# Block 4's scores, K^T V and state moved behind the second unit of products

## The chip, the cores and the metric

The kernel runs on one core of one Trainium2 chip. The metric is the device time of one execution in microseconds (us). Before the change it is 753.96 us, the median of three runs (753.72 to 754.04).

## What is computed

Two stages follow each other. The first is retention, a causal attention without softmax whose scores decay with the distance; the second is a feed-forward layer with the maximum of three products in its middle.

```python
scores = q @ k.T / sqrt(64)                      # batch 8, heads 8, sequence 576, head size 64
ret = scores * gamma[h] ** (i - j)  where i >= j, else 0
x = (ret @ v), heads side by side                # 4608 tokens x 512
h = maximum(maximum(x @ w1, x @ w2), x @ w3)     # 4608 x 768
out = h @ w_out                                  # 4608 x 512
```

All is float32 but the four weight matrices, which come as 64-bit floats and are taken apart into float32 on the chip.

## The kernel before

**Tiles.** The 4608 tokens are 36 blocks of 128, and four blocks are one tile of 512 tokens, so there are nine tiles. For a block, retention needs: its q, k and v loaded; v scaled by decay factors on GpSimd (`decay`, L243); q and k transposed (`transposes`, L256: on TensorE against the identity for the first blocks, into two PSUM banks `kt` and `qt` which ScalarE copies to SBUF at L274); the scores (`scores`, L276: 16 matmuls into two PSUM banks, s0 and s1, which VectorE multiplies by the causal mask into `st`); K^T V (`state`, L346: 8 matmuls recorded as 16 rows, into one bank `kv`); and the running state (`keep`, L357: VectorE reads `kv`, scales or adds it). `values` (L377) then multiplies the masked scores by v, adds the part of the state, and VectorE writes the result into `xT`, the input of the feed-forward layer, tile by tile.

**PSUM.** Three pools share it. `ps_r` has four buffers and serves retention: transposes, scores, K^T V and values. `ps_x` and `ps_y` have two each and serve the products of the feed-forward layer. Each buffer holds 512 float32 values per partition. A tile taken from a pool waits until an earlier holder has been read for the last time.

```python
    ps_r = ctx.enter_context(tc.tile_pool(name="ps_r", bufs=4, space=PSUM))
```

**The first tile.** While tile 0 runs through the feed-forward layer, the weights are still being loaded and converted. Its products come in nine units, three for each pair of 128 weight columns: pair 0 with w1, w2, w3, then pair 1, then pair 2. A unit is two calls of `up_plain` (L781), one for each column block; each is four products of 128 x 512 (recorded as eight rows, L786). The first result of a pair is copied to `h` by ScalarE (L793), the second and third are joined by VectorE's maximum (L791). The conversion of the weights is a generator (`convert_all`, L616) that hands out one step at a time: VectorE cuts out exponent and fraction (L632, L641), ScalarE makes the low word and the power of two (L634, L640, L643), VectorE puts fraction and sign in (L646, L650) and multiplies (L658). Each finished piece asks for one more piece from HBM (L661), so the 'bits' arrive in the order of the pieces, all over one DMA queue. The first three pairs of pieces (one pair for each unit) are converted one piece at a time, 128 x 512; from the fourth on two together, 128 x 1024. In the second unit `ffn` (L818) emits four conversion steps between a product and its maximum:

```python
                for fb in (2 * fp, 2 * fp + 1):
                    maximum, = up_plain(t, h, fb, i)
                    ...
                        convert(4 if (fp, i) == units[1] else 2)
                        maximum()
```

**The order of the work.** The tool that builds the program keeps the order in which the code emits instructions (L124), so every engine works through its instructions in program order. The order around the change is written out by hand in `steps` (L942): a list of 12 places for each tile, where retention of the next tile is dealt out; after each place `ffn` emits its next unit (L986 to L989). For tile 0 the first unit is `first_ups` (L800), which also holds block 3's values, then block 4's `decay` and `transposes`. In the lines of `steps` for t == 1, a is block 4, b block 5, c block 6 and d block 7. Place 1 holds block 4's scores, K^T V and state and lies between the first unit and the second; place 2 holds block 5's transposes and lies between the second and the third.

Of the kernel before, what the change touches and what calls it, by code (L numbers as in the profile page):

```python
# [81 lines left out]
def kernel(  # L82
# [698 lines left out]
    def up_plain(t, h, fb, i, *parts):  # L781
        ps = (ps_x, ps_y)[fb % 2].tile([P, NT], FP32, tag="xy"[fb % 2], name="up")

        def products(a, b):
            for dc in range(NDC):
                nc.tensor.matmul(ps[:, a:b], lhsT=w_sb[i, fb][:, dc * P:(dc + 1) * P], rhs=xT[t][:, dc, a:b],  # L786
                                 start=dc == 0 and a == 0, stop=dc == NDC - 1, skip_group_check=len(parts) > 0)

        def maximum():
            if i > 0:  # L790
                nc.vector.tensor_tensor(h[:, fb, :], h[:, fb, :], ps[:], op=ALU.max)  # L791
            else:
                nc.scalar.copy(h[:, fb, :], ps[:])  # L793

        ends = [0, *parts, NT]
        steps = [partial(products, a, b) for a, b in zip(ends, ends[1:])]
        steps.pop(0)()
        return (*steps, maximum)
# [143 lines left out]
    def steps(t):  # L942


        todo = [[] for _ in range(3 * CPT)]

        def at(n, *what):
            for step, *args in what:
                if step is values:
                    if args[0][0] < NG:  # L950
                        todo[n].append(partial(values, *args))
                elif args[0] < NG:
                    todo[n].append(partial(soon, partial(step, *args)) if step is load else partial(step, *args))

        if t == 1:
            a, b, c, d = range(CPT, 2 * CPT)
            at(0, (load, b))
            at(1, (scores, a), (state, a), (keep, a))
            at(2, (transposes, b), (decay, b), (load, c), (load_weights, 2))
            at(3, (scores, b), (load_blocks, d, 0))  # L960
            at(4, (decay, c), (load_blocks, d, 1, 2))
            at(5, (values, [a, b], [b, c]), (load_blocks, d, 3), (load, d))
            at(6, (keep, c), (transposes, c), (load_blocks, d + 1, 0))
            at(7, (transposes, d), (decay, d), (load_blocks, d + 1, 1, 2))
            at(8, (scores, c), (scores, d), (load_blocks, d + 1, 3), (load, d + 1))
            at(9, (load_blocks, d + 2, 0, 1))
            at(10, (decay, d + 1), (load_blocks, d + 2, 2))
            at(11, (values, [c, d], [d]), (load_blocks, d + 2, 3), (load, d + 2),
               (transposes, d + 1))
            return todo  # L970
        for n in range(0, CPT, 2):
            a, b, m = CPT * t + n, CPT * t + n + 1, 6 * (n // 2)
            first_pair = a == BY_CHUNKS
            s = m + 2 if first_pair else m + 1
            at(m - (t == 2 and n > 0), (transposes, b))
            if first_pair:
                at(m, (decay, b), (load, a + 2), (carry, a))
            at(s, (scores, a), (scores, b), (load, b + 2))
            at(s + 1, (decay, a + 2))
            at(s + 2, (decay, b + 2))  # L980
            at(s + 3, (values, [a, b]), (transposes, a + 2), (load, a + 4))
        return todo

    for t in range(N // NT):
        work = ffn(t)
        for todo in steps(t + 1):  # L986
            for step in todo:
                step()
            next(work, None)  # L989
# [51 lines left out]
```

## Time and profile before

| what | value |
|---|---|
| time, median of 3 | 753.96 us |
| span of the profiled execution | 751.6 us |
| granted TensorE clock, mean | 1.00 |
| TensorE matmul rows of 'up' (L786, all tiles) | 208 rows, 563 ns mean length (they overlap) |
| share of the chain in lines L762 (later tiles' products) | PE a 19%, b 16%, c 8%, d 5%, e 5% |
| DMA busy share, by tens of us | 0.9 or more in each of the first six, 0.61 in the seventh |

The profile names engines PE (TensorE; PEld is its weight load), DVE (VectorE), ACT (ScalarE), POOL (GpSimd) and SP (the queue that issues the transfers). A row of a timeline gives the start and length in us, the engine, the line, the operation, the tiles written and read, how many instructions are merged, and in brackets the idle time of the engine before it with what ended it. A busy TensorE row's end is a model; its start is not.

### The profile page before, as it was taken

What the parts mean: (1) busy time and instruction counts of PE and PEld (TensorE: products, weight loads), DVE (VectorE), ACT (ScalarE), POOL (GpSimd) and SP (SyncE); (2) the same over time, 40 slices, a digit from 0 to 9 for tenths busy, and PEclk for the clock granted to TensorE, in tenths of its full rate; (3) what the DMA queues carried; (4) which work ended last, traced back from release to release, by engine and by line L of the source; (5) the groups of instructions that cost most, each with busy time, mean ns of one, the idle gap of its engine ahead of it and who ended that gap; (6) DMA issues with size and microseconds to landing.
All of it is one profiled execution on the core that took longest, in us unless ns stands there. A gap on an engine that the chain in (4) does not pass through costs nothing.

```text
span 751.6 us, 16577 instructions
## 1 busy us (share of the span) xinstructions
PE 744.8 (99%) x6736; PEld 609.4 (81%) x6736; DVE 509.9 (68%) x856; ACT 319.7 (43%) x645; POOL 83.1 (11%) x103
## 2 busy tenths in 40 slices
PE   8999999999999999999999999999999999999998
PEld 7645545588888888888888888888888888888887
DVE  3997987857866765686567746775667656763662
ACT  3754531155245433644254335542554245414441
POOL 3210112002000100011010101010101010100000
PEclk9999999999999999999999999999999999999999
DMA  9995842515152414242333224232424141000001
GB/s 227 229 248 132 227 88 73 96 17 99 44 94 41 87 48 97 47 77 52 81 78 67 62 66 91 48 67 67 88 38 92 44 93 37 1 30 29 0 1 57
DMA packets 230204, 59.30 MB, mean 79 GB/s; under 512 B 210800, under 2 KB 228848, under 8 KB 230128
## 3 DMA queue, kind: packets, MB, share of 16 engines
q1 hardware_dynamic: 228720, 57.91, 35.4%
q8 instruction: 53, 0.87, 0.5%
q10 hardware_dynamic: 1408, 0.33, 0.2%
q14 instruction: 23, 0.19, 0.1%
HBM read 48.76 MB, written 9.44 MB: 77 GB/s over the span
## 4 chain that ended last, share of the span: by engine, by line
PE 97%; DMA 1%; SPq 1%; ACT 0%; DVE 0%; issue 0%
PE a L762 19%; PE b L762 16%; PE dx L559 11%; PE up L786 11%; PE c L762 8%; PE dz L559 6%; PE d L762 5%; PE e L762 5%; PE sk L309 3%; PE down L773 3%; PE dy L559 3%; PE o L426 2%; PE o L433 2%; PE s L287 1%; PE o L395 1%; PE kv L312 1%
## 5 line engine op out<-in xcount | busy, mean ns | idle before, releaser
L750 DVE TENSOR_TENSOR part<-part 128x512 f32<-128x512 f32 x161 | 111.2, 691 | 107.6 <-ACT part L747 105.2
L747 ACT COPY part<-b 128x512 f32<-128x512 f32 x115 | 67.3, 585 | 154.9 <-PE b L762 154.9
L750 DVE TENSOR_TENSOR h<-h,part 128x512 f32<-128x512 f32 x115 | 79.5, 691 | 29.1 <-ACT h L747 25.2
L786 PE MATMUL up<-xT,w 128*128 128x512 f32 (+2 forms) x208 | 84.8, 563 | 0.0
L747 ACT COPY part<-a 128x512 f32<-128x512 f32 x92 | 53.8, 585 | 49.4 <-PE a L762 48.9
L786 PEld LDWEIGHTS up<-xT,w 128*128 128x128 f32 x208 | 37.7, 190 | 41.4 <-issue 38.4
L762 PE MATMUL a<-s,w 128*128 128x256 f32 x276 | 70.9, 380 | 0.0
L762 PE MATMUL b<-s,n 128*128 128x256 f32 x276 | 70.8, 379 | 0.0
L191 ACT ACTIVATE vraw<-vraw,gk 128x64 f32<-128x64 f32 x208 | 65.5, 346 | 1.5 <-DMA vraw<-in_v_dram 1.5
L762 PEld LDWEIGHTS b<-s,n 128*128 128x128 f32 x276 | 52.5, 190 | 7.1
L762 PEld LDWEIGHTS a<-s,w 128*128 128x128 f32 x276 | 52.4, 190 | 7.1
L529 POOL TENSOR_TENSOR H<-h 128x256 f32<-128x256 f32 x24 | 20.2, 841 | 310.1 <-DVE h L750 310.1
L762 PE MATMUL c<-xT,w 128*128 128x256 f32 x184 | 49.1, 389 | 0.0
L762 PE MATMUL d<-s,w 128*128 128x256 f32 x184 | 47.2, 379 | 0.0
L762 PE MATMUL b<-xT,n 128*128 128x256 f32 x184 | 47.2, 379 | 0.0
L326 POOL TENSOR_TENSOR s<-s,gs_of 64x512 f32<-64x512 f32 x21 | 22.4, 1068 | 211.2 <-DVE s L324 209.2
L559 PE MATMUL dx<-To,H 128*128 128x256 f32 (+1 forms) x204 | 44.9, 370 | 0.0
L762 PE MATMUL e<-xT,w 128*128 128x256 f32 x184 | 43.5, 379 | 0.0
L762 PE MATMUL a<-xT,n 128*128 128x256 f32 x184 | 43.5, 379 | 0.0
L559 PEld LDWEIGHTS dx<-To,H 128*128 128x128 f32 x204 | 36.7, 190 | 4.8
L762 PEld LDWEIGHTS e<-xT,w 128*128 128x128 f32 x184 | 35.0, 190 | 5.1 <-DVE s L324 0.2
L762 PEld LDWEIGHTS d<-s,w 128*128 128x128 f32 x184 | 35.0, 190 | 4.7
(122 smaller groups left out, 1287.3 us busy)
## 6 DMA issues: line engine op xcount, KB each, us to landing
bits<-in_moe_w_dram SPq DMA_DIRECT2D x36, 256.0 KB, 5.7
out_dram<-osb SPq DMA_DIRECT2D x35, 256.0 KB, 2.1
kraw<-in_k_dram SPq DMA_DIRECT2D x32, 256.0 KB, 3.1
vraw<-in_v_dram SPq DMA_DIRECT2D x32, 256.0 KB, 3.5
qraw<-in_q_dram SPq DMA_DIRECT2D x224, 32.0 KB, 2.2
kxraw<-in_k_dram SPq DMA_DIRECT2D x224, 32.0 KB, 2.1
bits<-in_moe_w_out_dram SPq DMA_DIRECT2D x6, 512.0 KB, 5.1
qraw<-in_q_dram SPq DMA_DIRECT2D x6, 256.0 KB, 5.8
```

The costliest lines, as they stand in the source:

```text
L191: scaling.popleft()()
L309: nc.tensor.matmul(s[half(c), h, :], lhsT=kT[half(c), h, :], rhs=qT[half(c), h, :], start=True, stop=True)
L326: nc.gpsimd.tensor_tensor(new, new, factor, op=ALU.mult)
L426: nc.tensor.matmul(o[m][half(c), n, u, :], lhsT=vds[g][half(m), h, :], rhs=sts[g][half(m), h, :], start=n == 0 and u == 0, stop=place(g, m ...
L433: nc.tensor.matmul(o[m][half(c), n, u, :], lhsT=stacks[g][half(m), h, :], rhs=qks[g]["q"][half(m), h, :], start=False, stop=True, skip_gro ...
L529: urgent.append(lambda: (pool(s3, a11, a21, op=ALU.subtract), pool(s4, a12, s2, op=ALU.subtract)))
L559: nc.tensor.matmul(o, lhsT=hS[n](fp)[:, m * P:(m + 1) * P], rhs=late["T"][n][:, fp, cols], start=first and fp == order[0] and (m == 0 or l ...
L747: nc.scalar.copy(of[step], ps[step[0]][:])
L750: nc.vector.tensor_tensor(of[dst], a, b, op=op)
L762: nc.tensor.matmul(ps[chain][:, e, :], lhsT=factor(w, 2 * fp + e), rhs=xS[t][x], start=n == 1 and e == 0, stop=ends, skip_group_check=True)
L773: nc.tensor.matmul(b[:], lhsT=h[:, fb, m * P:(m + 1) * P], rhs=w_sb["out", fb], start=(fb == 0), stop=(fb == NF - 1))
L786: nc.tensor.matmul(ps[:, a:b], lhsT=w_sb[i, fb][:, dc * P:(dc + 1) * P], rhs=xT[t][:, dc, a:b], start=dc == 0 and a == 0, stop=dc == NDC - ...
```

## The change

The list of place 1 is put at the head of place 2. Scores, K^T V and state of block 4 are then emitted after the second unit's products, conversions and maxima, directly ahead of block 5's transposes. Nothing else moves, and no instruction is added or removed. The second unit then stands between block 4's transposes, whose copies ScalarE has still to make, and the scores that read these copies.

```diff
         if t == 1:
             a, b, c, d = range(CPT, 2 * CPT)
             at(0, (load, b))
-            at(1, (scores, a), (state, a), (keep, a))
-            at(2, (transposes, b), (decay, b), (load, c), (load_weights, 2))
+            at(2, (scores, a), (state, a), (keep, a), (transposes, b), (decay, b), (load, c), (load_weights, 2))
             at(3, (scores, b), (load_blocks, d, 0))
```

## The prediction

> **What bounds the kernel now.** I read the page's busy table and chain first, to see whether any engine but TensorE can set the end.
>
> ```profile
> span 751.6 us, 16577 instructions
> ...
> PE 744.8 (99%) x6736; PEld 609.4 (81%) x6736; DVE 509.9 (68%) x856; ACT 319.7 (43%) x645; POOL 83.1 (11%) x103
> ...
> PE 97%; DMA 1%; SPq 1%; ACT 0%; DVE 0%; issue 0%
> ```
>
> TensorE is the chain. The question is then where it stands still, so I asked for its waits from 33 us to the end (columns: total us, times, longest). There is one answer:
>
> ```profile
> PE s L287 <- ACT qT L274: 0.8, 1, 0.8
> ```
>
> It lies at the place that the change touches: block 4's scores wait for the copy of its transposed q. After it TensorE never waits again. So nothing later can swallow a delay made here: a microsecond lost or won near 40 us arrives at the end whole. The timeline of TensorE around it (start, length, work, idle before) gives the order of the work:
>
> ```profile
> 31.70 0.60 PE L273 MATMUL kt<-ident,kraw 128*128 128x128 f32 x4
> 32.14 0.60 PE L273 MATMUL qt<-ident,qraw 128*128 128x128 f32 x4
> 33.52 1.16 PE L287 MATMUL s<-qT,kT 64*128 64x128 f32 x16 [0.78 <-ACT qT L274]
> 34.61 0.68 PE L354 MATMUL kv<-vd,kraw 64*64 64x64 f32 x16
> 35.22 7.13 PE L786 MATMUL up<-xT,w 128*128 128x512 f32 x16
> 42.19 0.60 PE L273 MATMUL kt<-ident,kraw 128*128 128x128 f32 x4
> 42.63 0.60 PE L273 MATMUL qt<-ident,qraw 128*128 128x128 f32 x4
> 43.07 7.03 PE L786 MATMUL up<-xT,w 128*128 128x512 f32 x16
> ```
>
> The fifth line is the second unit (columns 0 and 1 of the first weight pair, i = 1); the first two are block 4's transposes, the sixth and seventh block 5's. I use starts, since the ends overlap the next start. Pieces by starts: a set of four transposes 0.44 us (42.63 - 42.19), scores 1.09, K^T V 0.61, the unit 6.97 (42.19 - 35.22).
>
> The third thing to know is what VectorE does in that stretch, because it masks the scores. Its timeline:
>
> ```profile
> 34.80 1.28 DVE L203 TENSOR_TENSOR st<-s,causal 128x512 f32<-128x512 f32 x2
> 36.00 0.41 DVE L362 TENSOR_TENSOR state<-kv,gs 128x256 f32<-128x256 f32 x1
> ...
> 40.89 1.41 DVE L658 TENSOR_TENSOR w<-mant,expo 128x512 f32<-128x512 f32 x1
> 42.40 0.69 DVE L632 TENSOR_SCALAR expo<-bits 128x1024 int32<-128x1024 int32 x1
> 43.01 0.69 DVE L641 TENSOR_SCALAR frac<-bits 128x1024 int32<-128x1024 int32 x1
> 43.80 1.23 DVE L646 SCALAR_TENSOR_TENSOR mant<-frac,mant 128x1024 f32<-128x1024 int32 x1
> 44.95 0.68 DVE L791 TENSOR_TENSOR h<-h,up 128x512 f32<-128x512 f32 x1
> ```
>
> and ScalarE's row for the same weights, which waited for the transfer that brings them:
>
> ```profile
> 42.40 1.29 ACT L634 ACTIVATE mant<-bits,one 128x1024 f32<-128x1024 uint32 x1 [4.13 <-DMA bits<-in_moe_w_dram]
> ```
>
> The reader is to see two things. The masks stand ahead of the second unit's conversions on VectorE now. And the last conversions of that unit (L632, L641, L646 on 128x1024, the first piece pair of the next weight columns) can't begin before 42.40, when their bits land; only after them comes the unit's second maximum, L791 at 44.95, although its product was finished at about 42.3.
>
> **What the Trainium skill says.** "Perfetto Trace Analysis", section "Tensor Engine Instruction (MATMUL, LD_WEIGHTS)", says that ends of TensorE rows are estimated while ACT and DVE are strict FIFO. The trace agrees: TensorE's lengths overrun the next start (0.60 against 0.44), and the maximum at 44.95 stood behind conversions. "PSUM — Partial Sum Buffer", section "Specifications (TRN2)", gives eight banks of 512 fp32 values per partition. The kernel's pools take 4 + 2 + 2 of them; the trace shows no bank numbers. "TensorE: Matmul & The Clock Gate", section "Part 1: The HAM clock gate", says that an idle window of about 3.4 us, whose phase is free, halves the clock. In this trace four transposes took 1.06 us at 4.15 us and 0.60 at 31.70, so a slower start is there; a drop inside the run is not.
>
> **The change part by part.**
>
> *Removed: the wait of 0.78 us.* TensorE will go from block 4's transposes straight to the second unit. That needs the unit's weights: by the timeline of VectorE the product (L658) of its first column ended at 32.29 and of its second at 34.21. The transposes hand over at 32.14 + 0.44 = 32.58, and the second column is needed 3.5 us later, so neither is waited for. The output banks come from the other two pools and were free by then. Unit: 32.58 to 39.55. Scores: 39.55 to 40.64. K^T V: to 41.25. First half of block 5's transposes: to 41.69. Up to here TensorE is 42.63 - 41.69 = 0.94 us ahead of before (0.78 of wait and the pipeline's refill).
>
> *Moved: the masks and the state, on VectorE.* They leave their place at 34.80 and go behind all of the second unit's conversions and both its maxima. Nothing that stood behind them is late: the first five conversions come 1.6 us sooner, but end in a wait for the bits of 42.40. The transfers are issued in the same order and none of them waits on VectorE for its buffer until after that, so I take 42.40 unchanged. Then 43.01, 43.80, the maximum at 44.95, and the first mask 0.61 later (a maximum at 51.92 was followed by a mask at 52.52): 45.56 to 46.24.
>
> *Added: a wait for a bank.* The pool of scores, K^T V and transposes has four banks. Block 4's two score banks and its K^T V bank stay taken until VectorE has read them; the transposed k of block 5 takes the fourth. The transposed q of block 5 has no bank until the first mask is done. Before, that mask ended at about 35.5, seven microseconds before q's turn. Now it ends at 46.24; a release from VectorE to TensorE cost 0.05 us (a mask that ended at 18.00, matmuls at 18.05). So q's transposes start at 46.29 in place of 42.63: **3.66 us later**, a stall of 4.6 us from 41.69. Behind them in TensorE's queue stands everything: the third unit, block 5's scores, all later units; they wait with it.
>
> *Costs nothing:* the state update (0.41 us of VectorE) and the second mask follow the first mask while TensorE transposes and runs the third unit for 7 us. Two steps merging into one list adds no instruction. Block 4's masked scores and state are first used at 65.05. ScalarE copies block 5's q after 46.9 instead of 46.27; its scores come 7 us after. The conversions of the next columns end at about 50.3 in place of 49.5, but their unit starts at 51.12 + 3.66 = 54.8.
>
> Sum: 753.96 - 0.94 + 4.60 = 753.96 + 3.66 = **757.6 us**.
>
> **The rivals.**
>
> *Only the removed wait counts* (not slower). If a bank were free for q, or VectorE reached the masks before 42 us, the change would give its 0.94 us: 753.96 - 0.94 = 753.0, which is within 0.2%. For it speaks that TensorE shows no bank wait anywhere after 33 us. Against it: the count of four banks leaves no spare, and the conversion ahead of the masks has the transfer's wait in it. 0.07.
>
> *The bank wait and a slower clock after it.* A stall of 4.6 us exceeds the page's idle window of 3.4 us, and with a free phase holds a whole one in (4.6 - 3.4)/3.4 = 35% of the cases. By estimate from the page the work then runs at half speed for most of a window or two, which loses 1.2 to 3.4 us, most likely 1.6: 757.6 + 1.6 = 759.2. For: the four transposes at 4.15 took 1.06 us. Against: no lower clock within this span. 0.28.
>
> *A shorter bank wait.* If the bits land 2 us sooner than at 42.40, the stall shrinks alike: 755.6. DMA engines are busy throughout, and the issue order is the same, so there is little for it: 0.03.
>
> **How the numbers follow.** The full wait at full clock has 0.62 and is the forecast, 757.6. Its own uncertainty is the refill after a stall and the transfer's landing, some 0.5 us either way. The range 756.6 to 760.4 holds it and most of the slower clock; it leaves out the two smaller cases and the slower clock's tail, under 2 in 10. Slower by over 0.2% (beyond 755.5): 0.62 + 0.28 + most of 0.03, so 0.92. Within 0.2%: 0.06. Faster: 0.02, for a removed wait with a knock-on that I don't see.
>
> **What would show it.** In the changed profile: the second unit's products start near 32.6 with no wait; the scores near 39.6; an idle stretch of some 4.5 us on TensorE ahead of the transposed q of block 5, ended by VectorE's L203; the first mask near 45.6 right behind L791 at 44.95; the third unit near 46.7; no other new wait. A dip of the granted clock near 46 would be the slower rival. Without the idle stretch, or with the masks ahead of 42.4, the forecast is wrong.

## The result, and the profile after

| | before | after |
|---|---|---|
| time, median | 753.90 us (753.70 to 754.04, 6 runs) | 758.11 us (755.55 to 759.02, 6 runs) |
| ratio | | 1.0054, 95% interval 1.0039 to 1.0069 |
| span of the profiled execution | 751.6 us | 756.7 us (that execution took 759.02) |
| mean granted TensorE clock of that execution | 1.00 | 0.995 |

The change costs 4.2 us. The forecast was 757.6, with a range of 756.6 to 760.4. Where the time went shows in three views. First the waits of TensorE from 30 us to the end (total us, times, longest), which have a single answer again, but another than before:

```profile
PE qt L273 <- ACT kT L274: 3.1, 1, 3.1
```

The timeline of TensorE shows where it lies:

```profile
31.66 0.60 PE L273 MATMUL kt<-ident,kraw 128*128 128x128 f32 x4
32.09 0.60 PE L273 MATMUL qt<-ident,qraw 128*128 128x128 f32 x4
32.53 7.03 PE L786 MATMUL up<-xT,w 128*128 128x512 f32 x16
39.49 1.16 PE L287 MATMUL s<-qT,kT 64*128 64x128 f32 x16
40.58 0.68 PE L354 MATMUL kv<-vd,kraw 64*64 64x64 f32 x16
41.20 0.66 PE L273 MATMUL kt<-ident,kraw 128*128 128x128 f32 x4
44.98 1.11 PE L273 MATMUL qt<-ident,qraw 128*128 128x128 f32 x4 [3.13 <-ACT kT L274]
45.88 9.31 PE L786 MATMUL up<-xT,w 128*128 128x512 f32 x16
55.12 1.16 PE L287 MATMUL s<-qT,kT 64*128 64x128 f32 x16
```

The second unit follows block 4's transposes without the old wait, and block 5's k is transposed at 41.20, 0.99 us sooner than before. Then TensorE stands still for 3.1 us, counted from the modelled end of that row, until block 5's q may be transposed. From there two rows are longer than before: q's transposes take 0.90 us from start to start in place of 0.44, and the third unit 9.24 in place of 6.96. The windows of one us say why (each row gives the window and its length, the busy time of PE, PEld, DVE, ACT and POOL with the number of instructions after x, then the granted clock, the DMA share and GB/s):

```profile
43.00:44.00 1.00, 0.00 (x0) 0.00 (x0) 1.00 (x2) 0.97 (x2) 0.00 (x0) 0.82 1.04 249
44.00:45.00 1.00, 0.02 (x1) 0.02 (x1) 1.00 (x3) 0.93 (x2) 0.00 (x0) 0.50 1.07 270
...
49.00:50.00 1.00, 1.00 (x2) 0.34 (x1) 0.00 (x0) 1.00 (x2) 0.00 (x0) 0.50 1.06 239
50.00:51.00 1.00, 1.00 (x3) 0.53 (x2) 0.00 (x0) 1.00 (x2) 0.00 (x0) 0.77 1.09 245
```

The clock fell to half during the stall and came back near 50.5. The sum closes: q starts 2.35 us later than before (44.98 - 42.63), its transposes lose 0.46 and the third unit 2.28, so block 5's scores start 5.09 us later (55.12 - 50.03). The profiled execution took 759.02, which is 5.06 above the 753.96 of the profiled execution before. Nothing after 55 us gave any of it back.

Last, the other two engines. VectorE:

```profile
40.98 0.69 DVE L632 TENSOR_SCALAR expo<-bits 128x1024 int32<-128x1024 int32 x1 [0.21 <-DMA bits<-in_moe_w_dram]
41.59 0.69 DVE L641 TENSOR_SCALAR frac<-bits 128x1024 int32<-128x1024 int32 x1
42.38 1.23 DVE L646 SCALAR_TENSOR_TENSOR mant<-frac,mant 128x1024 f32<-128x1024 int32 x1
43.52 0.68 DVE L791 TENSOR_TENSOR h<-h,up 128x512 f32<-128x512 f32 x1
44.12 1.28 DVE L203 TENSOR_TENSOR st<-s,causal 128x512 f32<-128x512 f32 x2
```

and ScalarE:

```profile
40.97 1.26 ACT L634 ACTIVATE mant<-bits,one 128x1024 f32<-128x1024 uint32 x1 [2.90 <-DMA bits<-in_moe_w_dram]
42.13 1.14 ACT L640 ACTIVATE expo<-expo,top 128x1024 f32<-128x1024 int32 x1
43.30 1.15 ACT L643 ACTIVATE expo<-expo,inf 128x1024 int32<-128x1024 f32 x1
44.36 0.57 ACT L274 COPY kT<-kt 128x512 f32<-128x512 f32 x1
```

Both stood behind the conversions that wait for their bits, as forecast. But the first mask ended near 44.80 (44.12 and 0.68 for one of the two) and the copy of block 5's k at 44.93, and q started at 44.98: the profile names the copy as the releaser. The built programs agree. The first matmul of q's transposes waits for a transfer and for one engine, and that engine changed from VectorE (DVE) to ScalarE (Activation):

```
-L273 Matmult qt<-ident,qraw 128x128 [waits DMAHW0_49,DVE_49]
+L273 Matmult qt<-ident,qraw 128x128 [waits DMAHW0_49,Activation_49]
```

In the kernel before, q got a bank of block 4's scores; after the change the builder gave it the bank of its own block's k, so it waits until ScalarE has copied k out.

### The profile page after: what moved, and what is told of

It reads as the page before. It is cut to its first block, busy times and chain, and to the rows that moved or that the text cites. A ratio compares the mean times of both kernels' runs of the same rounds, so it can differ in the third digit from the quotient of the medians.

```text
span 756.7 us, 16578 instructions
## 1 busy us (share of the span) xinstructions
PE 747.9 (99%) x6736; PEld 610.1 (81%) x6736; DVE 510.4 (67%) x856; ACT 319.6 (42%) x645; POOL 83.8 (11%) x103
## 4 chain that ended last, share of the span: by engine, by line
PE 96%; SPq 2%; DMA 1%; ACT 1%; issue 0%; DVE 0%; POOL 0%; POOLq 0%; ACTq 0%
PE a L762 18%; PE b L762 16%; PE dx L559 11%; PE up L786 9%; PE c L762 8%; PE dz L559 5%; PE e L762 5%; PE d L762 5%; PE sk L309 3%; PE down L773 3%; PE dy L559 3%; PE o L426 2%; PE o L433 2%; SPq L241 1%; PE o L395 1%; PE s L287 1%
## 5 line engine op out<-in xcount | busy, mean ns | idle before, releaser
L786 PE MATMUL up<-xT,w 128*128 128x512 f32 (+2 forms) x208 | 87.0, 575 | 0.1
L762 PEld LDWEIGHTS b<-xT,n 128*128 128x128 f32 x184 | 35.0, 190 | 4.8
```

The lines of the kernel that those rows point to most:

```text
L762: nc.tensor.matmul(ps[chain][:, e, :], lhsT=factor(w, 2 * fp + e), rhs=xS[t][x], start=n == 1 and e == 0, stop=ends, skip_group_check=True)
```

## The experiments

The comparisons are with the kernel before, run on the same chip beside each. It took 753.97 us beside the first filler, the bank for q, the copies first and the masks first; 753.95 beside the changed kernel run again, the second filler, the late conversion and the scores moved alone; 754.18 beside the other three. A ratio stands with its 95% interval. Two questions were open: how much of the 4.2 us is the stall and how much the clock, and what it is that q waits for.

### The clock: keep TensorE busy in the stall

In `transposes`, with FILLER = 15:

```diff
+            if g == CPT + 1 and n == "q":
+                warm(FILLER)
             pt = pool.tile([P, NP, C], FP32, tag=tag, name=n + "t")
```

> The changed kernel with fifteen extra products of the identity with itself on TensorE ahead of block 5's q transposes (into a bank of the third pool that is free; their result is used by nobody, the rest is computed as before). At full clock two recorded rows of 0.11 us are one such product, so they fill 3.3 of the 3.8 us of the stall and don't move its end. Theory 'the stall also costs clock': the granted clock stays 1.0, the third unit takes 7.0 us in place of 9.3, and the time is 753.9 + 2.3 = 756.2, some 2 us less than the changed kernel's 758.1. Rival 'the whole loss is the wait, and the clock costs nothing': 758.1 as without the filler.

Measured: 757.58 us, ratio 1.0047 (1.0034 to 1.0059), clock 1.00 in all five runs. The clock behaved as its theory says, but the time was 1.4 us above the expected. In the profiled execution the bits landed only at 42.82, and q started at 46.87 in place of 44.98. So executions and chips differ in the landing, and the comparison needed the changed kernel on the same chip:

> The changed kernel once more, beside the one with the filler. Theory 'the stall also lowers the clock': above the filler's time of the same chip by 1.2 to 2.7 us (one to two windows of 3.4 us at half speed, less what falls into the stall), and the profile shows a stretch at 0.50 after the stall and a third unit of more than 7.1 us. Rival 'the loss is the wait alone, and only the landing of the bits makes runs differ': the same time as with the filler within 0.4 us.

> As the filler before, now beside the changed kernel on the same chip: fifteen products of the identity ahead of block 5's q transposes, of which nobody uses the result. Theory 'the stall also lowers the clock': clock 1.0, and 1.2 to 2.7 us below the changed kernel. Rival 'the loss is the wait alone': no difference. In both, q starts about 4 us after k.

Measured on one chip: 758.51 us without the filler (1.0067, 1.0054 to 1.0080), 756.80 with it (1.0040, 1.0027 to 1.0052). All five runs without it had a mean clock of 0.995 to 0.998, all with it 1.00, so the filler kept the clock up. The medians differ by 1.7 us. As the clock's part this is a rough figure: there are five runs of each, and the landing moves by more than a microsecond (in the two profiled executions the bits landed at 42.37 and 41.09, so q started 5.28 us after k without the filler and 4.07 with it, where some 4 had been expected in both). Within one trace the clock's part does not hang on the landing. From start to start, against the kernel before, q's transposes and the third unit lost 0.46 and 1.06 us in this profile of the changed kernel, 1.5 us together, and 2.7 us (0.46 and 2.28) in the first. What is left with the filler, 2.85 us (756.80 - 753.95), is put down to the stall. The filler itself ends near 45.1 and can't show a stall shorter than that. The timelines of TensorE show both parts. Without the filler:

```profile
41.13 0.66 PE L273 MATMUL kt<-ident,kraw 128*128 128x128 f32 x4
46.41 1.12 PE L273 MATMUL qt<-ident,qraw 128*128 128x128 f32 x4 [4.61 <-ACT kT L274]
47.31 8.08 PE L786 MATMUL up<-xT,w 128*128 128x512 f32 x16
55.33 1.16 PE L287 MATMUL s<-qT,kT 64*128 64x128 f32 x16
```

With it (the lines of this kernel are numbered three higher):

```profile
41.09 0.66 PE L276 MATMUL kt<-ident,kraw 128*128 128x128 f32 x4
41.58 3.51 PE L159 MATMUL warm<-ident 128*128 128x128 f32 x30
45.16 0.66 PE L276 MATMUL qt<-ident,qraw 128*128 128x128 f32 x4
45.65 7.03 PE L789 MATMUL up<-xT,w 128*128 128x512 f32 x16
52.62 1.16 PE L290 MATMUL s<-qT,kT 64*128 64x128 f32 x16
```

The third unit is 8.08 long where the clock is lowered for a part of it, and 7.03 at full clock. The start of q follows the landing: in the changed kernel's two profiles ScalarE's L634 began at 40.97 and 42.37 and q at 44.98 and 46.41; in the two filler profiles at 42.81 and 41.09, and q at 46.87 and 45.16. Always 4.0 to 4.1 us lie between, the three activations and the copy.

### A bank for q

```diff
             pool, tag = (ps_r, "r") if g >= CPT else (ps_x, "x")
+            if g == CPT + 1 and n == "q":
+                pool, tag = ps_y, "y"
```

> The changed kernel, but the transposed q of block 5 is put in a bank of the third pool, which is free at that time. Nothing in the order of any engine changes: the masks and the copy of the transposed k still come after the conversions that wait for their bits. Theory 'q waits for a bank and for nothing else': no stall above 0.2 us ahead of q, clock 1.0, and the gain of the removed wait alone: 753.9 - 0.9 = 753.0. Rival 'q waits for its data or for VectorE's or ScalarE's work itself': a stall of 3 to 4 us stays, 757 to 758.

Measured: 753.58 us, ratio 0.9995 (0.9986 to 1.0003). No order was touched, VectorE masked at 45.66 and ScalarE copied k at 45.91, as late as ever, yet q went right behind k. So the bank is what q waits for. Of the 0.9 us that should be won, 0.4 arrived, and the interval holds 1, so even that is not clear of noise. The one wait that is left on TensorE tells where the rest went (lines numbered two higher; the wait is of the fifth unit, at 58.06):

```profile
PE up L788 <- DVE w L660: 0.4, 1, 0.4
```

That unit came 0.4 us too soon for its converted weights: from start to start, it began 7.52 us after the fourth (50.54) in place of 6.97.

### Which release: the copy of k, or the masks

Both pieces were emitted ahead of the second unit's last four conversion steps, one at a time; TensorE's order is that of the changed kernel in each. The steps so moved are taken out of the list of places, which the excerpts below do not show. In `ffn`, behind the product of the unit's second column, the copies first (the masks are held back until after the maximum):

```diff
+                    if (fp, i) == units[1] and fb % 2:
+                        spread.append(True)
+                        for step in (scores, state, keep):
+                            step(CPT)
+                        spread.clear()
+                        transposes(CPT + 1)
...
                         maximum()
+                        chore(len(urgent))
```

> The changed kernel, with block 4's scores and K^T V and block 5's transposes emitted ahead of the second unit's last four conversion steps, but the masks and the state update left behind them. TensorE's order is that of the changed kernel; ScalarE copies the transposed k of block 5 ahead of the conversions that wait for the bits; VectorE masks as late as in the changed kernel. Theory 'ScalarE's copy of k gives the bank that q waits for' (the trace names it): q starts 0.6 us after k's transposes, near 42.3, third unit right behind: 753.9 - 0.3 = 753.6, clock 1.0. Rival, the forecast's own 'VectorE's first mask gives the bank': the stall stays, 757 to 758.

Or the masks first, with the transposes left in place 2:

```diff
+                    if (fp, i) == units[1] and fb % 2:
+                        scores(CPT)
+                        state(CPT)
+                        keep(CPT)
```

> The changed kernel, with block 4's scores, K^T V, masks and state update emitted ahead of the second unit's last four conversion steps. TensorE's order is that of the changed kernel; VectorE masks before the conversions that wait for the bits; ScalarE copies the transposed k of block 5 as late as in the changed kernel. Theory 'any of the four banks will do, the first to be read': q takes a bank of the scores, whose mask ends near 41.3, and does not stall: 753.0, plus up to 1 us because VectorE now stands idle for the scores and its conversions come 2 us later than before, so 753.0 to 754.0. Rival 'only ScalarE's copy of k frees q's bank': the stall stays, 757 to 758.

Measured: copies first 754.86 us (1.0014, 1.0007 to 1.0020), masks first 754.07 (1.0002, 0.9993 to 1.0010). With the copies first, q keeps k's bank and starts behind the copy, four microseconds ahead of the masks. TensorE, then VectorE:

```profile
41.26 0.66 PE L273 MATMUL kt<-ident,kraw 128*128 128x128 f32 x4
42.59 0.66 PE L273 MATMUL qt<-ident,qraw 128*128 128x128 f32 x4 [0.68 <-ACT kT L274]
```

```profile
46.77 1.28 DVE L196 TENSOR_TENSOR st<-s,causal 128x512 f32<-128x512 f32 x2
```

With the masks first, the program gives q a bank of the scores; q started at 42.23, although ScalarE copied k only at 48.20. So either release will do, and in the changed kernel it was the copy.

Neither kernel gained in the end. With the copies first, q started at 42.59, as in the kernel before (42.63): the wait for the copy, which was expected, took back what the removed wait gave. The rest was lost to the weights of the fourth and fifth unit. VectorE masked only at 46.77, after a conversion that stood 1.74 us waiting for ScalarE, and came late with what those units need:

```profile
51.44 7.13 PE L786 MATMUL up<-xT,w 128*128 128x512 f32 x16 [0.23 <-DVE w L658]
58.76 7.13 PE L786 MATMUL up<-xT,w 128*128 128x512 f32 x16 [0.19 <-DVE w L658]
65.82 1.97 PE L395 MATMUL o<-st,vd 128*64 128x128 f32 x32
```

The idle times in brackets, from modelled ends, show about half of it. From start to start the fourth unit came 1.39 us after block 5's scores (50.05) in place of 1.09, and the values 14.38 after the fourth unit in place of 13.93 (65.05 - 51.12). That is 0.75 us, nearly all of the 0.79 by which the profiled execution (754.75) was longer than that of the kernel before. With the masks first, VectorE stood idle for 2.64 us waiting for the scores, and the fourth and fifth unit waited 0.86 and 0.65 us for L658 in the profiled execution, which at 755.41 was the slowest of its thirteen.

### The conversion that waits for its transfer

```diff
-                        convert(4 if (fp, i) == units[1] else 2)
+                        convert(4 if (fp, i, fb) in ((0, 1, 0), (0, 2, 0)) else 2)
```

> The changed kernel with the two conversion steps that wait for the bits moved from the second unit's second column to the third unit's first column, behind the masks, the state and the transposes' copies. Theory 'the transfer of the bits, ahead of the masks and the copy in VectorE's and ScalarE's order, makes the stall': q's bank is one of the scores', read near 42, so q waits 0.4 us at most: 753.4 to 754.0 (the upper end if the conversions of later units keep TensorE waiting as in the kernel with the masks first). Rival 'masks behind the second unit are late whatever stands ahead of them': a stall of over 2 us, above 756.

Measured: 753.41 us, ratio 0.9992 (0.9983 to 1.0000). The stall is gone, with the masks at 40.70 and the copy of k at 41.65, and q is not held up (the third row starts 0.49 behind the second):

```profile
40.35 0.68 PE L354 MATMUL kv<-vd,kraw 64*64 64x64 f32 x16
40.96 0.66 PE L273 MATMUL kt<-ident,kraw 128*128 128x128 f32 x4
41.45 0.64 PE L273 MATMUL qt<-ident,qraw 128*128 128x128 f32 x4
41.93 7.03 PE L786 MATMUL up<-xT,w 128*128 128x512 f32 x16
```

So the move behind the second unit is harmless by itself. It hurts because two conversion steps stand in front of what releases the banks. They delay the release by their wait for the transfer and by their own work, and this experiment takes both away together. The wait is not all of it. In the first profile of the changed kernel VectorE stood only 0.21 us for the bits (L632 at 40.98; 2.45 us in the second), and from there ScalarE needed 3.4 us for its three activations before it could copy k.

I also tried to bring the transfer forward by loading block 5's v one place later (`(load, b, "kq")` at place 0, `(load, b, "v")` at place 1):

> The changed kernel with block 5's v loaded one place later, so that the bits that VectorE and ScalarE wait for are issued ahead of it. Theory 'q starts 4.0 us after the bits land, or after VectorE comes to them': VectorE comes to them near 40.0, the two activations that need it end near 43.0, the copy of k near 43.6, and q starts there in place of 45 to 46.4: a stall of some 2 us, [...] 753.95 + 1.0 = 755.0. Rival 'the transfer has no part in it': 758 to 759, clock below 1.

Measured: 759.13 us (1.0063, 1.0051 to 1.0076), a miss. L634 began at 42.06 and q started at 46.06, again 4.0 later, but the bits were not clearly sooner: measured from block 4's transposes they landed at +9.8 us, which lies between the +9.3 and +10.8 of the two profiles of the changed kernel. I had reckoned with the 3.35 us for which the issuing queue was busy with v. At its new place the same issue took 0.55 us, so most of that time was not v's own; v is 256 KB, and at the some 250 GB/s of these microseconds that is 1.0 us by estimate. The stall, 3.57 us, was still long enough to lower the clock, as in all five runs of this kernel. The time is the one that the rival named, and the experiment doesn't decide between the two: in the trace the stall followed the transfer, but the transfer was not moved enough.

### One part of the change at a time

K^T V and the state stay, the scores move:

```diff
+            at(1, (state, a), (keep, a))
-            at(2, (scores, a), (state, a), (keep, a), (transposes, b), (decay, b), (load, c), (load_weights, 2))
+            at(2, (scores, a), (transposes, b), (decay, b), (load, c), (load_weights, 2))
```

> The changed kernel, but K^T V and the state update stay ahead of the second unit; only the scores of block 4 move behind it. TensorE makes K^T V while ScalarE copies q. Theory 'four banks, all taken, make the stall': K^T V's bank is read before 37, so q has a bank although the masks and k's copy are as late as in the changed kernel; no stall, clock 1.0, 753.0 and up to 0.4 us more if a later unit waits for its weights. Rival 'moving the scores is enough for the stall': 757 to 759.

The scores stay, K^T V and the state move:

```diff
+            at(1, (scores, a))
-            at(2, (scores, a), (state, a), (keep, a), (transposes, b), (decay, b), (load, c), (load_weights, 2))
+            at(2, (state, a), (keep, a), (transposes, b), (decay, b), (load, c), (load_weights, 2))
```

> The other half alone: block 4's scores stay ahead of the second unit, only K^T V and the state update move behind it. Theory 'four banks, all taken': the scores' banks are read before 36, so q has a bank; the wait of 0.8 us for the copy of q comes back; 753.95, the same as before within 0.4 us. Rival 'K^T V behind the unit is enough for the stall': 757 to 759.

Nothing moves behind the unit, but K^T V goes ahead of the scores:

```diff
-            at(1, (scores, a), (state, a), (keep, a))
+            at(1, (state, a), (scores, a), (keep, a))
```

> The kernel before, with K^T V of block 4 ahead of its scores instead of after them; nothing is moved behind the second unit. TensorE makes K^T V (0.6 us) while ScalarE copies q. Theory 'the wait for the copy is all that is to be had here': 753.95 - 0.6 = 753.3 to 753.4. Rival 'what TensorE wins here it loses to the next wait for weights': 753.8 to 754.0, with a wait for VectorE's L658 in a later unit.

Measured: 753.28 us for the first (0.9991, 0.9984 to 0.9997), 754.26 for the second (1.0002, 0.9993 to 1.0010), 753.41 for the third (0.9990, 0.9983 to 0.9996). Neither half makes the stall; only both together fill the four banks. With the scores alone behind the unit, VectorE masked at 44.60 and ScalarE copied k at 44.42, but K^T V's bank was free:

```profile
33.02 0.68 PE L354 MATMUL kv<-vd,kraw 64*64 64x64 f32 x16
33.63 7.13 PE L786 MATMUL up<-xT,w 128*128 128x512 f32 x16
40.69 1.16 PE L287 MATMUL s<-qT,kT 64*128 64x128 f32 x16
41.78 0.66 PE L273 MATMUL kt<-ident,kraw 128*128 128x128 f32 x4
42.28 0.60 PE L273 MATMUL qt<-ident,qraw 128*128 128x128 f32 x4
```

The same profile shows what the conversions cost without any wait for bits on VectorE. It came to them right behind its own work, and the copy of k, 2.95 us later, would by estimate have held q back by 2.7 us (44.99 - 42.28), had q needed that bank:

```profile
41.47 0.69 DVE L632 TENSOR_SCALAR expo<-bits 128x1024 int32<-128x1024 int32 x1
44.42 0.57 ACT L274 COPY kT<-kt 128x512 f32<-128x512 f32 x1
```

The first and the third are faster than the kernel before, by 0.7 and 0.8 us, and than the changed one: K^T V needs no q and fills most of the time in which ScalarE copies it.

## Why the prediction was right, and where it was not

**The removed wait** was right: 0.94 us worked out, 0.99 measured at k's transposes.

**The four banks** were right in the count. Freeing any one of them, by another pool, an early copy, early masks or an early K^T V, took the long stall away.

**"The transposed q of block 5 has no bank until the first mask is done"** is the step that failed. The mask was only one of the ways to a bank. The program gave q the bank of its own k, which ScalarE frees, so the sign that was named, an idle stretch ended by VectorE's L203, did not come. The prediction left that copy out of its count, although the trace before has it:

```profile
45.81 0.56 ACT L274 COPY kT<-kt 128x512 f32<-128x512 f32 x1
```

It ends at 46.37, and the mask was worked out to end at 46.24. That the number of the stall came out all the same is luck: the copy stands behind the same bits on ScalarE as the mask does on VectorE, and in the first profile both ended within 0.2 us of each other (44.93 and about 44.80). With bits at 42.37, in the second profile of the changed kernel, q started at 46.41; the prediction had 46.29.

**"I take 42.40 unchanged"** is right in the middle and too sure. The order of the transfers did not change, but the start of L634 lay between 40.97 and 42.81 in the profiles of the changed kernel and the filler, and the time moved with it. The shorter bank wait, which had 0.03 and 755.6, was therefore too lightly dismissed: one of the first six runs of the changed kernel took 755.55 at a clock of 1.00. It has no trace, so that its bits landed early is likely and not shown.

**The clock** was mis-weighted. The likeliest case had full clock at 757.6, and the lowered clock had 0.28 and 759.2. Five of the first six runs of the changed kernel had a mean clock below 1 and so had all five on the second chip. The size of the term was well estimated (1.6 us; 1.5 and 2.7 in the two traces, 1.7 between the medians with and without the filler). That the measured 758.11 lies so near to the 757.6 of the full clock is in part luck: on the second chip the stall was shorter than worked out (2.85 us net in place of 3.66), and the lowered clock, which the forecast left out, added 1.7. An idle window of 3.4 us was taken from the Trainium skill's "TensorE: Matmul & The Clock Gate", section "Part 1: The HAM clock gate", as the condition, and a chance of 35% from the stall's length. The first trace of the changed kernel differs from the page. There the clock fell about 1.8 us after the last transposes of k (43.6 against 41.86), so less than a whole window of idle time was enough. Why is not shown; the work just ahead was the small products of the scores, K^T V and transposes. In the second trace, where the drop came at 46.0 after 4.2 us without a matmul, a whole idle window fits ahead of it. The slow transposes near 4 us, which were counted for a slower clock, are no clear evidence: the granted clock reads 1.00 there too.

**"Nothing later can swallow a delay made here"** held: the 5.09 us at block 5's scores are 5.06 at the end. The clause after it claimed the same of a microsecond won, and that failed. Conversions of weights stand close behind TensorE, and with a bank of its own for q some 0.5 of the 0.9 us won were spent ahead of the fifth unit, waiting for L660.

## What to carry to other kernels

When work is moved back past other work, ask not only what it waits for but what it holds: here two scores banks and a K^T V bank stayed taken through two weight conversions and the wait for their bits, which had nothing to do with them. Count the buffers at the next request, and look at every engine that could free one, for what stands ahead of the release in its queue. Here a stall on TensorE of three to five microseconds cost 1.5 to 2.7 us more than its length, because the clock fell. A small wait for a copy was better filled by an independent product (K^T V ahead of the scores, 0.8 us won) than by moving the waiting work far away.

## What the runs showed of the hardware that was not expected

The lowered clock came in stretches of 3.4 us, in the second profile of the changed kernel and in the one with v loaded later, and of 6.8, twice that, in the first. A window reads 0.50 where the clock was lowered throughout and 1.00 where it was full, so a mean between gives the moment at which it changed. Two windows of half a microsecond from the second profile:

```profile
46.00:46.50 0.50, 0.10 (x1) 0.10 (x2) 0.50 (x2) 0.35 (x1) 0.00 (x0) 0.51 1.09 258
49.00:49.50 0.50, 0.50 (x2) 0.34 (x1) 0.50 (x1) 0.50 (x2) 0.00 (x0) 0.57 1.28 269
```

A mean of 0.51 puts the drop right behind 46.0, and one of 0.57 puts the return at 49.4. In the first profile, 0.82 in the window from 43 and 0.77 in that from 50 give 43.6 and 50.5. The clock fell with stalls of 3.1, 3.6 and 4.6 us in the traces, and not with one of 1.2, which the filler left. In the first profile it fell when TensorE had been idle for 1.8 us only, after 2.4 us of scores, K^T V and transposes.
